# Attention, experts and channel mix on one core: row sums from a column of ones, float32 probabilities for the whole first token tile, overlapping query columns, and new order tables

## The chip, the cores and the metric

The kernel runs on one core of a Trainium2 chip. It is one program that works on five engines: PE (TensorE, the matrix multiplier; its weight loads, which overlap its multiplies, are listed as PEld), DVE (VectorE), ACT (ScalarE), POOL (GpSimd) and SP (SyncE, which here only starts DMA transfers). Each engine runs its own queue of instructions in order and waits at semaphores for the others. The metric is the device time of one execution in microseconds (us).

## The reference, cut to what matters

Three layers follow each other on 2 batches of 768 tokens. The first is attention with 8 heads of 64 columns, in which a token sees only the keys that fall in its own hash bucket; the second a mixture of 4 experts, each a causal attention of its own; the third a channel mix with a shift by one token.

```python
# 1. bucketed attention: q, k, v are (2, 8, 768, 64), proj is (64, 6)
mask = q_bucket[:, :, :, None] == k_bucket[:, :, None, :]   # bucket: signs of q @ proj, k @ proj
scores = where(mask, 0.125 * q @ k.T, -1e9)
attn = exp(scores - max(scores)); attn = attn / (sum(attn) + 1e-09)
x = attn @ v                                                # heads side by side: (2, 768, 512)
# 2. four experts, each token takes two of them with weights w
a = exp(causal scores of x @ wq[e], x @ wk[e] - max); a /= sum(a) + 1e-09
out += w * (a @ (x @ wv[e]) @ wo[e])
# 3. channel mix, xk and xr mix a token with the one before it by mu_k, mu_r
k = maximum(xk @ w_k, 0); v = k * k @ w_v                   # w_k 512x1024, w_v 1024x512
return sigmoid(xr @ w_r) * v                                # w_r 512x512
```

## The kernel before

**Tiles.** The 1536 tokens are 12 tiles of 128 (i = 0 to 11, six to a batch). Each tile goes through the three layers in turn: for each of the 8 heads a score matrix of 128 tokens by 768 keys (`s`), its exponentials (`P`), and the product with the values (`x`); then the expert projections (`qk`, `vg`), the expert scores (`se`), their exponentials (`P_m` for one expert, `P_m_p` for two side by side) and products (`y`, `o`); then the channel mix (`h` hidden, `r` gate, `v` down), and a store to `out`.

**Numbers in two halves.** To keep float32 accuracy at 16-bit matmul speed, a float32 tile is split into a 16-bit "hi" part and the 16-bit rest "lo". Keys, queries, values and all weights are split this way when they are first used (`nak`, `nbk` for keys, `naq`, `nbq` for queries, `v` for values, and for weights `raw`, `wd`, then `WK`, `WV`, `WR`). A hi part is a copy that ACT, DVE or POOL can make; a lo part is a subtraction on DVE or POOL.

**One head of the attention.** PE multiplies `s`. DVE scales it into `P` and takes the row maximum `mx` in the same instruction (TENSOR_SCALAR_CACHE_REDUCE). ACT takes the exponential in place, and its `accum_out` gives the row sum `sm` (a second instruction, ACTIVATION_READ_ACCUMULATOR, follows each). ACT or POOL makes the hi half `PHL`, POOL the lo half, one DMA transpose on SP's queue turns both into `PT`, and PE multiplies 18 times per head with 64 columns of values. For eight pairs of tile and head (the set `F32T`) it goes another way: PE turns `P` in float32 by six transposes (`tp`), ACT copies them out of PSUM (`PF`), and PE multiplies in float32; no half, no DMA transpose. When all heads of a tile are done, DVE adds 1e-9 to the eight sums, takes reciprocals, and multiplies all 512 columns by them (`x32`, shown as `x<-x,rs`); PE then turns `x32` (`tr_x<-ident,x`) for the expert projections.

**What sets the order.** Nothing is issued where it stands in the code. A recorder (`Program`) keeps every instruction as an operation; a long table (ORDER) gives the order of issue, a second one (HOMES) the buffer of each tile, and a third (ENGINES) the engine of each hi part. All are then issued by one function, and so every row of the profile has line L225; the rows are told apart by tile names. Within an engine the order is fixed, so an instruction that waits holds up all that stand behind it.

**Start.** SP issues the loads of keys, queries and weights in the order of the table. The ACT queue issues the small ones: the projection twice (`pr32`, upper and lower 64 rows), `mur` and `muk` (512 numbers each, scattered one by one over 128 rows), the constants (identities and causal mask) and `ties`. ACT's first table load of an activation function stands behind these.

Of the kernel before, what the change touches and what calls it, by code (L numbers as in the profile page):

```python
# [25 lines left out]
SMQ = 64.0  # L26
# [20 lines left out]
F32T = {(i, h) for i in range(4) for h in (0, 1)}  # L47
# [205 lines left out]
def tile_lsh_moe_mix(  # L253
# [61 lines left out]
    consts = cp.tile([P, 3 * P], F16, name="consts")  # L315
    nc.scalar.dma_start(consts, consts_in[:, :3 * P])
    ident16 = consts[:, :P]
    ident = consts[:, P:2 * P].bitcast(BF16)
    causal = consts[:, 2 * P:3 * P].bitcast(BF16)
    ident32 = cp.tile([P, P], F32, name="ident32")  # L320
    nc.gpsimd.tensor_copy(ident32, ident16)
    pr32 = cp.tile([P, NB], F32, name="pr32")
# [5 lines left out]
    ties = cp.tile([P, E, E], F32, name="ties")  # L328
    muk = cp.tile([P, NC], F32, name="muk")
    mur = cp.tile([P, NC], F32, name="mur")  # L330

    def late_consts():
        nc.scalar.dma_start(ties, ties_in)
        nc.gpsimd.tensor_scalar(ties, ties, -(2.0 ** -120), 1.0, op0=OP.mult, op1=OP.mult)
        nc.scalar.dma_start(muk, mu_k.rearrange("(c p) -> p c", p=P))
        nc.scalar.dma_start(mur, mu_r.rearrange("(c p) -> p c", p=P))
# [18 lines left out]
    def turn(dst, src, nm, by_dma=False, engs="vv"):  # L355
# [4 lines left out]
        n = src.shape[1] // P  # L360
# [6 lines left out]
        for j in range(2):  # L367
            for c in range(hn):
                nc.tensor.transpose(pt[j][:, c * P:(c + 1) * P], src[:, (j * hn + c) * P:(j * hn + c + 1) * P], ident16)
# [104 lines left out]
    def key_steps(b, g):  # L474
# [4 lines left out]
        def load():  # L479
# [3 lines left out]
            st["v"] = kp.tile([P, 2, G, NT, D], F16, tag="v", name=f"v_{nm}")  # L483
# [3 lines left out]
        def half(j):  # L487
# [25 lines left out]
        def vals(j):  # L513
# [6 lines left out]
            vh, vl = st["v"][:, 0, 2 * j:2 * j + 2], st["v"][:, 1, 2 * j:2 * j + 2]  # L520
# [8 lines left out]
    NBQ = cp.tile([P, H, P], F16, name="nbq")  # L529
    nc.gpsimd.memset(NBQ[:, :, D + 2 * NB:], 0.0)  # L530

    def query_steps(i):
# [4 lines left out]
        def prep():  # L537
# [3 lines left out]
            st["na"] = na = sp.tile([P, H, P], F16, tag="b2", bufs=NB2, name=f"naq_{i}")  # L541
            nb = NBQ
            nc.scalar.activation(na[:, :, :D], q32, AF.Copy, scale=SQ)
            nc.vector.scalar_tensor_tensor(na[:, :, D:], q32, SQ, na[:, :, :D], op0=OP.mult, op1=OP.subtract)
# [502 lines left out]
```

## Time and profile before

| | before |
|---|---|
| median of 3 runs | 453.11 us (453.09 to 453.51) |
| the profiled execution, device time | 451.91 us |
| its span in the profile | 450.1 us (1.8 us lie around it) |
| busy PE / PEld | 419.1 us (93%) / 323.0 us (72%) |
| busy DVE / ACT / POOL | 350.3 (78%) / 317.9 (71%) / 349.7 us (78%) |
| TensorE clock granted | 1.00 of full speed in every stretch, which is 2.4 GHz |
| read / written in device memory | 22.14 MB / 3.15 MB |

Busy time is the time in which an engine has at least one instruction in work. On PE, where one multiply begins before the last has ended, the time from start to start tells more than the length of one. The sums further on are made against the profiled execution; the median of the runs lies 1.20 us above it.

### The profile page before, as it was taken

The page shows a single profiled execution, that of the slowest core. Times are in us where ns is not written, and L with a number is a line of the kernel's source. Part 1 is how long each engine was busy: PE and PEld are TensorE (multiplying, and loading weights), DVE is VectorE, ACT ScalarE, POOL GpSimd, SP SyncE. Part 2 cuts the span into 40 slices and gives each one's busy share as a digit, 9 for nine tenths or more (in the row PEclk, how much of TensorE's full clock was granted, in tenths as well). Part 3 has the DMA queues.
Part 4 walks back from the last instruction along what each step waited for, and adds up shares of the span by engine and source line. Part 5 has one row for each costly group of instructions (what it writes and reads, how often), then busy time and mean ns, then how long its engine had stood idle before and what let it go on. Part 6 is the DMA issues. An engine that isn't in the chain of part 4 may idle for free.

```text
span 450.1 us, 14852 instructions
## 1 busy us (share of the span) xinstructions
PE 419.1 (93%) x5984; PEld 323.0 (72%) x5984; DVE 350.3 (78%) x900; ACT 317.9 (71%) x617; POOL 349.7 (78%) x364
## 2 busy tenths in 40 slices
PE   0776798999999999999999999999999999999996
PEld 0655686888787677885778778777678868577672
DVE  1999999999999888998878878768758765655522
ACT  2898999998988795877786666668667636662220
POOL 4898998998999786899988899978987953844020
PEclk9999999999999999999999999999999999999999
DMA  8989999999999999498899999997998885328201
GB/s 247 233 234 221 251 207 243 196 194 257 199 161 212 192 220 229 107 169 145 144 158 199 184 155 198 179 161 114 188 158 161 125 146 83 83 58 169 60 1 70
DMA packets 227157, 75.54 MB, mean 168 GB/s; under 512 B 218512, under 2 KB 222736, under 8 KB 227088
## 3 DMA queue, kind: packets, MB, share of 16 engines
q1 hardware_dynamic: 225584, 74.48, 87.9%
q8 instruction: 47, 0.77, 0.7%
q10 hardware_dynamic: 1504, 0.11, 0.2%
q14 instruction: 22, 0.18, 0.1%
HBM read 22.14 MB, written 3.15 MB: 56 GB/s over the span
## 4 chain that ended last, share of the span: by engine, by line
PE 69%; DVE 11%; POOL 3%; issue 3%; ACT 2%; DMA 1%; DVEq 0%; POOLq 0%; ACTq 0%
PE v L225 13%; PE h L225 11%; PE x L225 9%; PE s L225 9%; PE r L225 6%; PE qk L225 6%; PE o L225 4%; DVE P L225 3%; PE se L225 3%; PE vg L225 3%; PE y L225 3%; DVE v L225 2%; POOL PHL L225 1%; PE tr_y L225 1%; DMA PT<-PHL 1%
## 5 line engine op out<-in xcount | busy, mean ns | idle before, releaser
L225 POOL TENSOR_TENSOR PHL<-P,PHL 128x768 f16<-128x768 f32 x88 | 146.7, 1674 | 9.5 <-ACT PHL L225 3.6
L225 ACT ACTIVATE P<-P,mx 128x768 f32<-128x768 f32 x96 | 89.2, 931 | 20.4 <-DVE P L225 16.9
L225 DVE TENSOR_SCALAR_CACHE_REDUCE P<-s 128x768 f32<-128x768 f32 x96 | 90.7, 950 | 8.3 <-PE s L225 6.0
L225 PE MATMUL s<-y,x 128*128 128x384 f16 x384 | 76.3, 326 | 7.4 <-DVE P L225 3.7
L225 PE MATMUL h<-mk,WK 128*128 128x128 f16 x1152 | 75.0, 219 | 0.0
L225 PEld LDWEIGHTS <-WK 128*128 128x128 f16 x1152 | 67.9, 98 | 6.2 <-DVE lg L225 0.4
L225 PEld LDWEIGHTS <-PT 128*128 128x128 f16 x1584 | 54.5, 98 | 8.9 <-DMA PT<-PHL 2.2
L225 PE MATMUL x<-v,PT 128*128 128x64 f16 x1584 | 58.0, 193 | 1.9 <-DMA PT<-PHL 1.9
L225 PEld LDWEIGHTS <-x 128*128 128x128 f16 x480 | 38.0, 98 | 27.4 <-issue 7.3
L225 PE MATMUL v<-WV,k2h 128*128 128x512 f16 x192 | 57.1, 379 | 0.0
L225 POOL TENSOR_SCALAR PHL<-P 128x768 f16<-128x768 f32 x50 | 42.8, 858 | 7.3 <-ACT P L225 4.1
L225 POOL TENSOR_TENSOR PHL_m<-P_m,PHL_m 128x512 f16<-128x512 f32 (+2 forms) x24 | 33.5, 1405 | 8.9 <-ACT PHL_m L225 8.4
L225 PE MATMUL r<-WR,mr 128*128 128x512 f16 x144 | 36.0, 379 | 0.8 <-DVE k2l L225 0.8
L225 PE MATMUL qk<-xT,WQK 128*128 128x128 f16 x576 | 36.6, 219 | 0.1
L225 PE MATMUL v<-WV,k2l 128*128 128x512 f16 x96 | 36.4, 379 | 0.0
L225 ACT ACTIVATE t<-h 128x512 f32<-128x512 f32 x24 | 14.2, 594 | 28.0 <-PE h L225 27.9
L225 PEld LDWEIGHTS <-WQK 128*128 128x128 f16 x576 | 33.3, 98 | 1.0 <-DVE xT L225 0.4
L225 ACT ACTIVATE PHL<-P 128x768 f16<-128x768 f32 x38 | 31.6, 838 | 2.2 <-ACT P L225 0.9
L225 DVE SCALAR_TENSOR_TENSOR h<-h,t 128x512 f32<-128x512 f32 x24 | 16.7, 694 | 18.8 <-ACT t L225 18.7
L225 PEld LDWEIGHTS <-k2h 128*128 128x128 f16 x192 | 16.8, 98 | 13.8 <-issue 0.7
L225 ACT ACTIVATE P_m<-P_m,bias_m 128x512 f32<-128x512 f32 (+2 forms) x24 | 19.7, 821 | 8.7 <-DVE P_m L225 8.7
L225 ACT ACT_TABLE_LOAD x16 | 20.5, 1283 | 6.5 <-DMA pr<-in_proj_dram 5.0
(172 smaller groups left out, 882.9 us busy)
## 6 DMA issues: line engine op xcount, KB each, us to landing
raw_k<-in_moe_w_k_dram SPq DMA_DIRECT2D x8, 512.0 KB, 4.8
raw_v<-in_moe_w_v_dram SPq DMA_DIRECT2D x8, 512.0 KB, 4.4
k<-in_k_dram SPq DMA_DIRECT2D x8, 384.0 KB, 5.1
q<-in_q_dram SPq DMA_DIRECT2D x12, 256.0 KB, 4.7
v<-in_v_dram SPq DMA_DIRECT2D x8, 384.0 KB, 4.3
out_dram<-e SPq DMA_DIRECT2D x12, 256.0 KB, 2.6
raw_r<-in_moe_w_r_dram SPq DMA_DIRECT2D x4, 512.0 KB, 4.9
PT<-PHL SPq DMA_TRANSPOSE x88, 4.6
```

The source lines that it names most:

```text
L225: getattr(getattr(self.nc, engine), method)(*[real(a) for a in args], **{k: real(a) for k, a in kw.items()})
```

## The change

Six things change together.

- **Row sums.** The hi half of the values gets a column of ones beside each 64 columns of values (`vh`, and `vnh` for the experts), so that the matmuls with it have 65 columns and the row sum of the probabilities appears in PSUM beside the product. The exponentials lose `accum_out` (88 of 96 in the attention, all 48 of the experts). The normalisation reads the sums from PSUM, and is done in two halves of four heads (`fin_half`), each with a PSUM tile of its own.
- **Float32 heads.** `F32T` has heads 0 and 1 of tiles 0 to 3 before, and all 8 heads of tile 0 now.
- **Queries.** For tiles 0 to 7 one tile `NQ` holds lo, hi and hash marks side by side, and the two turned operands are overlapping columns of it. The hi half is copied once, not twice.
- **Constants.** Identities, mask and `ties` are built on POOL (memset and AFFINE_SELECT). `mu_k` and `mu_r` are loaded as rows of 128 numbers and turned by PE (`tr_mu`). The two loads of `pr32` stand together at the head of the ACT queue.
- **Last tile.** The down projection of tile 11 is done in two halves of 256 columns, each with its own product and store.
- **Tables.** ORDER, HOMES and ENGINES are new. ENGINES gives 52 of the attention's hi halves to ACT and 36 to POOL, where 38 and 50 stood.

```diff
-F32T = {(i, h) for i in range(4) for h in (0, 1)}
+F32T = {(0, h) for h in range(8)}
...
-    consts = cp.tile([P, 3 * P], F16, name="consts")
-    nc.scalar.dma_start(consts, consts_in[:, :3 * P])
...
+    def pattern(name, shape, dt, steps, rows, op, fill):
+        t = cp.tile(shape, dt, name=name)
+        nc.gpsimd.memset(t, 0.0)
+        nc.gpsimd.affine_select(t, t, pattern=steps, compare_op=op, fill=fill, base=0, channel_multiplier=rows)
+        return t
...
     def late_consts():
-        nc.scalar.dma_start(ties, ties_in)
...
-        nc.scalar.dma_start(muk, mu_k.rearrange("(c p) -> p c", p=P))
-        nc.scalar.dma_start(mur, mu_r.rearrange("(c p) -> p c", p=P))
+        rows = sp.tile([P, P], F32, tag="b2", bufs=NB2, name="mu_rows")
+        nc.scalar.dma_start(rows[0:NC, :], mu_k.rearrange("(c p) -> c p", p=P))
+        nc.scalar.dma_start(rows[NC:2 * NC, :], mu_r.rearrange("(c p) -> c p", p=P))
+        pt = dps("tr_mu")[:, :2 * NC]
+        nc.tensor.transpose(pt, rows[0:2 * NC, :], ident32[0:2 * NC, 0:2 * NC])
+        hi_part("a", mu, pt)
...
+            st["vh"] = kp.tile([P, G, NT, D + 2], F16, tag="vh", name=f"vh_{nm}")
+            nc.gpsimd.memset(st["vh"][:, :, :, D:], 1.0)
...
-            nc.scalar.activation(na[:, :, :D], q32, AF.Copy, scale=SQ)
-            nc.vector.scalar_tensor_tensor(na[:, :, D:], q32, SQ, na[:, :, :D], op0=OP.mult, op1=OP.subtract)
-            nc.gpsimd.tensor_scalar(nb[:, :, :D], q32, SQ, 1.0, op0=OP.mult, op1=OP.mult)
+            if i in QD:
...
+            else:
+                lo, hi = NQ[:, :, :D], NQ[:, :, D:2 * D]
+            hi_part("a", hi, q32, SQ)
+            lo_part("v", lo, q32, hi, SQ)
...
-            nc.scalar.activation(d, d, AF.Exp, bias=biases[r], scale=-1.0, accum_out=sms[r])
+            nc.scalar.activation(d, d, AF.Exp, bias=biases[r], scale=-1.0)
...
+            o1 = st["x"][:, hh, :]
             for t in range(NT):
-                nc.tensor.matmul(o, PT[:, t, :], kg["v"][:, 0, hh, t, :], start=(t == 0), stop=False)
+                nc.tensor.matmul(o1, PT[:, t, :], kg["vh"][:, hh, t, :D + 1], start=(t == 0), stop=False)
...
+        def fin_half(g):
...
+            nc.vector.tensor_scalar(rs, st["sm"][:, hs] if own[0] else x[:, :, D], 1e-9, 1.0, op0=OP.add, op1=OP.mult)
+            nc.vector.reciprocal(rs, rs)
+            nc.vector.tensor_tensor(st["x32"].rearrange("p (h d) -> p h d", d=D)[:, hs], x[:, :, :D],
+                                    rs.unsqueeze(2).to_broadcast([P, G, D]), op=OP.mult)
...
+        def down_half(j, f):
...
+            nc.vector.scalar_tensor_tensor(o, pv_, 1.0 / (ST * ST * SWV2), o, op0=OP.mult, op1=OP.mult)
+            LOADS.dma_start(out[b, s0:s0 + P, js], o)
...
 ORDER = """
-c-jrsg8~@F5&*!x-CJC2+qP}nwr$(CZ5wS+#6}z2DPlX#d-D^6&>jHVfC7OBg8)$=3sizwP!zI4IcNvjAR-7jXbTabB+P?oFaU}{RLB7gIiWa|hg?trazhE|4-23S{OY
```

What stands on the queues, read from the order of instructions. Names carry buffer numbers behind them, and a "32" in a name is left out (`x_3` below is `x32_3`).

The head of the ACT queue, before:

```order
L225 DMA pr_72<-in_proj_dram 64x6
L225 DMA mur<-in_moe_mu_r_dram 128x4x1
L225 DMA consts<-in_consts_dram 128x384
L225 DMA ties<-in_ties_dram 128x16
L225 DMA pr_72<-in_proj_dram 64x6
L225 ACT_TABLE_LOAD
L225 ACTIVATE nak_0_0_85<-k_0_0_0_80 128x12x64
```

and now:

```order
L225 DMA pr_77<-in_proj_dram 64x6 x2
L225 DMA mu_rows<-in_moe_mu_r_dram 4x128
L225 DMA mu_rows<-in_moe_mu_k_dram 4x128
L225 ACT_TABLE_LOAD
L225 ACTIVATE nbq<-q_0_100 128x8x64
L225 ACTIVATE wd_k_0_119<-raw_k_0_113 128x512
L225 ACTIVATE mu<-tr_mu 128x8
```

The second projection load moved from fifth place to second, three loads went, and the first copy is one of queries where it was one of keys.

The head of DVE's queue, before:

```order
L225 CAST prhl<-pr_72 128x6
L225 SCALAR_TENSOR_TENSOR nak_0_0_85<-k_0_0_0_80,nak_0_0_85 128x12x64
L225 SCALAR_TENSOR_TENSOR naq_103<-q_0_95,naq_103 128x8x64
L225 TENSOR_TENSOR prhl<-pr_72,prhl 128x6
L225 COPY x_0_136<-tr_x_0_130 128x512
```

and now:

```order
L225 CAST prhl<-pr_77 128x6
L225 TENSOR_TENSOR prhl<-pr_77,prhl 128x6
L225 SCALAR_TENSOR_TENSOR nbq<-q_0_100,nbq 128x8x64
L225 SCALAR_TENSOR_TENSOR wd_k_0_119<-raw_k_0_113,wd_k_0_119 128x512
L225 COPY x_0_129<-tr_x_0_106 128x512
L225 SCALAR_TENSOR_TENSOR wd_k_0_119<-raw_k_0_113,wd_k_0_119 128x512
L225 SCALAR_TENSOR_TENSOR nak_0_0_136<-k_0_0_0_132,nak_0_0_136 128x12x64
```

The cast of the projection still stands first; behind it queries and a weight now come ahead of the first keys.

DVE's queue from the end of tile 3's normalisation on, before (204 instructions stand ahead of the first row, from the top of the queue):

```order
L225 TENSOR_TENSOR x_3_2330<-x_2046,rs_2077 128x512
L225 TENSOR_SCALAR P_6_2337,mx_2126<-s_6_2316 128x768
L225 SCALAR_TENSOR_TENSOR WV_3_2340<-wd_v_0_2231,WV_3_2340 128x512
L225 TENSOR_TENSOR xT_2343<-tr_x_2332,xT_2343 128x512
L225 TENSOR_SCALAR P_m_p_2365,bias_m_2_2366<-se_1_2353 128x384
```

and now (200 stand ahead):

```order
L225 TENSOR_TENSOR x_3_2043<-x_0_2056,rs_2034 128x256
L225 TENSOR_SCALAR P_7_2239,mx_1962<-s_7_2182 128x768
L225 TENSOR_SCALAR lg_2253,gm_2254<-vg_2216 128x4
L225 SCALAR_TENSOR_TENSOR WV_1_2191<-wd_v_0_2041,WV_1_2191 128x512
L225 TENSOR_TENSOR xT_2276<-tr_x_2232,xT_2276 128x512
L225 SCALAR_TENSOR_TENSOR wd_r_0_2331<-raw_r_0_2107,wd_r_0_2331 128x512
```

The one multiply of 512 columns is now the second of two with 256, with four instructions fewer ahead of it; among these, the ones that split `w_v` and `w_r` (`wd_v`, `wd_r`, `WV`, `WR`) fell from 24 to 14.

## Rows read from the trace of the kernel before

**Rows 1.** Windows: stretch, length, busy of PE, PEld, DVE, ACT, POOL, clock, DMA.

```profile
10.00:40.00 30.00, 21.34 (x246) 16.48 (x247) 29.40 (x61) 26.82 (x48) 26.96 (x28) 1.00 0.99 225
40.00:80.00 40.00, 33.79 (x500) 27.91 (x500) 39.09 (x95) 36.93 (x82) 37.66 (x40) 1.00 1.13 231
80.00:120.00 40.00, 39.44 (x591) 33.98 (x589) 39.29 (x106) 38.14 (x84) 38.05 (x41) 1.00 1.08 215
120.00:180.00 60.00, 59.93 (x895) 45.96 (x893) 54.55 (x146) 48.77 (x93) 51.35 (x55) 1.00 1.08 204
```

**Rows 2.** Timeline 0 to 13 us: start us, us, engine, instruction.

```profile
0.72 0.55 ACTq L225 DMA_DIRECT2D pr<-in_proj_dram  x1
4.50 0.49 ACTq L225 DMA_DIRECT2D pr<-in_proj_dram  x1
10.04 0.37 DVE L225 CAST prhl<-pr 128x6 f16<-128x6 f32 x1 [10.04 <-DMA pr<-in_proj_dram]
10.14 0.96 DVE L225 SCALAR_TENSOR_TENSOR nak<-k,nak 128x768 f16<-128x768 f32 x1
11.16 0.82 PE L225 MATMUL tr_y<-consts,nak 128*128 128x128 f16 x6 [11.16 <-DMA w_qk<-in_moe_wk_dram]
```

**Rows 3.** Timelines around 99, 119 and 150 us: normalisation of tiles 2 to 4, its transposes.

```profile
99.72 0.64 PE L225 MATMUL tr_x<-ident,x 128*128 128x128 f32 x4
118.76 0.68 DVE L225 TENSOR_TENSOR x<-x,rs 128x512 f32<-128x512 f32 x1
119.73 0.60 PE L225 MATMUL tr_x<-ident,x 128*128 128x128 f32 x4
149.45 0.68 DVE L225 TENSOR_TENSOR x<-x,rs 128x512 f32<-128x512 f32 x1
161.47 0.60 PE L225 MATMUL tr_x<-ident,x 128*128 128x128 f32 x4
```

**Rows 4.** Page, part 6: DMA issues, KB each, us to landing.

```profile
k<-in_k_dram SPq DMA_DIRECT2D x8, 384.0 KB, 5.1
q<-in_q_dram SPq DMA_DIRECT2D x12, 256.0 KB, 4.7
```

**Rows 5.** Lines by form, DVE: count, busy us, mean ns, idle before.

```profile
L225 DVE TENSOR_SCALAR_CACHE_REDUCE P<-s 128x768 f32<-128x768 f32 x96 | 90.7, 950 | 8.3 <-PE s L225 6.0 <-ACT P L225 1.5 <-DMA PT<-PHL 0.2
L225 DVE SCALAR_TENSOR_TENSOR wd_v<-raw_v,wd_v 128x512 uint32<-128x512 uint32 x16 | 11.1, 692 | 0.8 <-issue 0.6
L225 DVE TENSOR_TENSOR x<-x,rs 128x512 f32<-128x512 f32 x12 | 8.2, 686 | 3.0 <-PE x L225 3.0
L225 DVE TENSOR_TENSOR y<-y,rse 128x256 f32<-128x256 f32 x12 | 5.0, 420 | 1.4 <-PE y L225 1.2
L225 DVE RECIPROCAL rs<-rs 128x8 f32<-128x8 f32 x12 | 2.4, 196 | 0.1
```

**Rows 6.** Timeline 108 to 113 us, DVE: how far one instruction overlaps the next.

```profile
109.05 0.41 DVE L225 TENSOR_SCALAR_CACHE_REDUCE P_m_p<-se 128x256 f32<-128x256 f32 x1
109.39 0.41 DVE L225 TENSOR_SCALAR_CACHE_REDUCE P_m_p<-se 128x256 f32<-128x256 f32 x1
```

**Rows 7.** Timeline 144 to 147.2 us, PE: runs of matmuls at full rate.

```profile
144.25 1.50 PE L225 MATMUL h<-mk,WK 128*128 128x128 f16 x24
146.24 1.16 PE L225 MATMUL x<-v,PT 128*128 128x64 f16 x34
```

**Rows 8.** Timeline 59.5 to 63 us, ACT: an exponential and two copies.

```profile
59.97 0.95 ACT L225 ACTIVATE P<-P,mx 128x768 f32<-128x768 f32 x1
60.88 1.58 ACT L225 ACTIVATE PHL<-P 128x768 f16<-128x768 f32 x2
```

**Rows 9.** Lines by form, ACT: the copies of turned float32 probabilities.

```profile
L225 ACT ACTIVATE PF<-tp 128x384 f32<-128x384 f32 x15 | 7.1, 485 | 0.1
```

**Rows 10.** Timeline 441 to 450.1 us: the end.

```profile
446.33 0.69 DVE L225 SCALAR_TENSOR_TENSOR e<-v,e 128x512 f32<-128x512 f32 x1 [1.96 <-PE v L225]
```

**Rows 11.** Tile nak: duration ns min/median/max of the DVE instruction.

```profile
L225 DVE SCALAR_TENSOR_TENSOR nak<-k,nak x8: 947/958/1571, 10.1 to 178.4; 128x768 f16<-128x768 f32 x8
```

More of the change, by code (lines that the diff above doesn't have):

```diff
@@ L359, in turn @@
             return
-        n = src.shape[1] // P
+        n = dst.shape[1]
         hn = n // 2
@@ L368, in turn @@
             for c in range(hn):
-                nc.tensor.transpose(pt[j][:, c * P:(c + 1) * P], src[:, (j * hn + c) * P:(j * hn + c + 1) * P], ident16)
+                t = j * hn + c
+                nc.tensor.transpose(pt[j][:, c * P:(c + 1) * P],
+                                    src[:, t, :] if len(src.shape) == 3 else src[:, t * P:(t + 1) * P], ident16)
             o, pj = dst[:, j * hn:(j + 1) * hn, :], pt[j].rearrange("p (n s) -> p n s", s=P)
@@ L528, in tile_lsh_moe_mix @@
     QX, QS_ = {}, {}
-    NBQ = cp.tile([P, H, P], F16, name="nbq")
-    nc.gpsimd.memset(NBQ[:, :, D + 2 * NB:], 0.0)
+    NQ = cp.tile([P, H, 3 * D], F16, name="nbq")
+    nc.gpsimd.memset(NQ[:, :, 2 * D + 2 * NB:], 0.0)
     def query_steps(i):
@@ L616, in score @@
             if h == 0:
-                st["sm"] = sp.tile([P, H], F32, tag="sm", name=f"sm_{i}")
+                if any((i, hh) in F32T for hh in range(H)):
+                    st["sm"] = sp.tile([P, H], F32, tag="sm", name=f"sm_{i}")
                 st["mx"] = sp.tile([P, H], F32, tag="mx", name=f"mx_{i}")
@@ L664, in lsh_steps @@
                 steps.append(lambda h=h: pv(h - LAG))
+            if h >= LAG and (h - LAG) % G == G - 1:
+                steps.append(lambda h=h: fin_half((h - LAG) // G))
         steps.append(lambda: fin())
@@ L684, in proj_qk @@
                 KV[b] = (kp.tile([P, 2, EP, S], F16, tag="kT", bufs=1, name=f"kT_{b}"),
-                         kp.tile([P, NT, 2, E * D], F16, tag="vn", bufs=1, name=f"vn_{b}"))
+                         kp.tile([P, NT, E, D + 2], F16, tag="vnh", bufs=1, name=f"vnh_{b}"),
+                         kp.tile([P, NT, E, D], F16, tag="vnl", bufs=1, name=f"vnl_{b}"))
+                nc.gpsimd.memset(KV[b][1][:, :, :, D:], 1.0)
             kT = KV[b][0]
@@ L739, in proj_v @@
             nc.gpsimd.tensor_scalar(gs, gs, 1e-9, 1.0, op0=OP.add, op1=OP.mult)
-            st["sm"] = sp.tile([P, E], F32, tag="sme", name=f"sme_{i}")
         def score(c):
@@ L775, in score @@
                 es = (2 * c, 2 * c + 1)
-                PT = softmax_pair(Sv, n, 0.125 / (SMQ * SMQ), [st["sm"][:, e:e + 1] for e in es],
+                PT = softmax_pair(Sv, n, 0.125 / (SMQ * SMQ),
                                   [sp.tile([P, 1], F32, tag="bias", bufs=4, name=f"bias_m{i}_{e}") for e in es],
@@ L904, in gate @@
                 nc.scalar.activation(e, pr, AF.Sigmoid, scale=1.0 / (SX2 * SWR))
+        def down_half(j, f):
+            need(W)
+            js = slice(j * DM // 2, (j + 1) * DM // 2)
+            if f == 0:
+                st["pv"] = dps(f"v_{i}_{j}", [P, DM // 2])
+            pv_, k2 = st["pv"], st["k2"]
+            nc.tensor.matmul(pv_, k2[0][:, f, :], WV2[f][:, 0, js], start=(f == 0), stop=False)
+            nc.tensor.matmul(pv_, k2[0][:, f, :], WV2[f][:, 1, js], start=False, stop=False)
+            nc.tensor.matmul(pv_, k2[1][:, f, :], WV2[f][:, 0, js], start=False, stop=(f == NF - 1))
+            if f < NF - 1:
+                return
+            o = st["e"][:, js]
+            nc.vector.scalar_tensor_tensor(o, pv_, 1.0 / (ST * ST * SWV2), o, op0=OP.mult, op1=OP.mult)
+            LOADS.dma_start(out[b, s0:s0 + P, js], o)
         def down(f):
@@ L921, in mix_steps @@
                                   + [lambda c=c: gate(c) for c in range(NC)]
-                                  + [lambda f=f: hidden(f) for f in range(4, NF)] + [lambda f=f: down(f) for f in range(NF)])]
+                                  + [lambda f=f: hidden(f) for f in range(4, NF)]
+                                  + ([lambda f=f: down(f) for f in range(NF)] if i < NU - 1 else
+                                     [lambda j=j, f=f: down_half(j, f) for j in range(2) for f in range(NF)]))]
     W = weight_steps()
```

206 lines of the change are left out of this document (107 added, 99 removed).

## The prediction

> **What bounds the kernel now.** I read the windows by stage first. From 80 us on PE is busy nearly all the time, 39.44 of 40 us and then 59.93 of 60 us, while in 10 to 40 us it is busy 21.34 of 30 and in 40 to 80 us 33.79 of 40 [rows 1]. DVE is the reverse: 29.40 of 30, 39.09 of 40 and 39.29 of 40 us up to 120, then 54.55 of 60. So there are two regimes. Until about 120 us DVE never rests and sets the pace; after that PE never rests, and an instruction saved elsewhere buys nothing. The clock granted to PE is 1.00 in every stretch, so no clock enters the sum.
>
> Next the timeline, for where each regime begins. DVE's first instruction is the cast of the projection, at 10.04 us, and it waits for the second projection load, which the ACT queue issues only at 4.50 us; DVE's next, the lo part of the first keys, follows at 10.14, and PE's first transpose at 11.16 [rows 2]. The wait table puts PE's 11.16 us down to a weight load, but the transposes read `nak`, whose lo part ends at 11.10; it is DVE that released it.
>
> Then the seam. Normalisation of tile 3 on DVE runs from 118.76 for 0.68 us, and PE starts the transposes that need it at 119.73, 0.29 us after its end. Tile 2's transposes start at 99.72. Tile 4's normalisation ends at 150.13, but PE only comes to it at 161.47, so 11.3 us of slack lie there [rows 3]. Tile 3 is thus the last delivery of DVE for which PE waits long. The end moves by what PE's waiting up to tile 3's transposes loses, which is how much earlier DVE delivers, less how much less work PE has ahead of it, unless tile 4 then comes late.
>
> **The start.** The ACT queue now issues four loads of a few rows, the two projections first, at 0.72 and, by the 0.55 us of the first issue, about 1.3 us, in place of 4.50 [rows 2]. DVE can cast at some 6 us. What it does next hangs on loads: the first queries are now first on SP's queue (5.4 us by the 0.72 of an issue and the 4.7 to landing, then a hi copy on ACT, under the 0.73 of a wider one [rows 8]), then a weight, then keys, which land some 5.1 us after an issue [rows 4]. The first keys are now third on SP's queue, at about 1.7 us, so land at about 7 and are ready in both halves near 9, by which time DVE has some 3 us of work behind it. Before, the first useful work began at 10.14 with 0.1 us of work behind it. I bound the gain between 3 us (the third and fourth pair of keys land one after the other, and DVE waits once more) and 5.5 us (it never waits), and take 4.0. PE's first instruction is now a transpose of the `mu` rows, which waits for the fourth load of the ACT queue, issued by about 2.9 us and landing by 8.0 if a few rows take as long as keys do; then the query transposes start there and the gain is at its low end. Building constants on POOL costs two AFFINE_SELECTs that the trace does not show, between nothing and the 0.95 us of the longest instruction in [rows 8] each; POOL had nothing to do then but memsets, and PE needs the identity only near 6 us, so I take nothing.
>
> **DVE's work up to tile 3.** By the order, 204 instructions stand ahead of the last multiply of tile 3's normalisation before, 200 now. I price each by its mean less 0.07 us, since one of 0.41 us starts 0.34 us after the last [rows 6].
> - The splits of `w_v` and `w_r` fall from 24 to 14: 10 x 0.62 = -6.2 us (0.692 less 0.07) [rows 5]. They are not gone, but done later.
> - One block of the channel mix (`h`, `k2l`) and one cast of `xT`, 512 wide, move behind: 3 x 0.62 = -1.9. Two reductions `P_m_p` of 384 columns move behind: between the 0.42 of 256 and the 0.69 of 512 columns, 2 x 0.48 = -1.0.
> - Three reductions of `P` come ahead: 3 x 0.88 = +2.6 [rows 5].
> - Normalisation in halves: 8 multiplies of 256 columns (0.420 less 0.07) for 4 of 512 (0.686 less 0.07), +0.3; 8 sums and 8 reciprocals for 4 and 4, at 0.1 to 0.2 us each [rows 5], +1.2.
> - Four more copies of transposes (+1.5) and some ten fewer small instructions (-1.5) cancel.
>
> The sum is -5.0 us; with the start, tile 3 is delivered 9.0 us earlier. The same list for tile 2 gives +0.4, so 3.6 earlier.
>
> **PE's work up to there.** Ahead of tile 3's transposes PE has 48 hidden matmuls fewer. 24 take 1.50 us, of which the last hangs over by some 0.2, so one costs about 0.056: -2.7. Eight score matmuls of 384 columns come ahead, eight expert scores and 16 small transposes and hash products go: +1.3 - 1.1 - 0.6. A matmul of 64 columns costs (1.16 - 0.19) / 33 = 0.0294, one of 128 0.0557, so 0.41 ns for a column [rows 7]. In all -2.9 us. PE's waiting up to tile 3 falls by 9.0 - 2.9 = 6.1 us. At tile 2 it falls by 3.6 + 1.6 = 5.2, since PE has 1.6 us more to do there. Between those two transposes PE spent 20.0 us [rows 3] on 18.4 us of work, so tile 2 was 1.6 us less tight, and tile 3 still decides.
>
> **What stands next to be late.** By the order PE has 18.9 us less work ahead of tile 4's transposes (96 hidden, 20 score, 24 output matmuls and others moved behind them) and DVE 10.8 us less. PE gets there at 161.47 - 18.9 - 6.1 = 136.5, DVE delivers at 150.13 - 10.8 - 4.0 = 135.3. The 11.3 us of slack shrink to 1.2, enough if each step holds.
>
> **What PE does more.** 1392 matmuls get a 65th column (1056 of 1584 in the attention, 336 of 504 in the experts). The trace has none of 65; one costs between a 64 column matmul and a 128 column one, 0 to 26 ns more, so 0 to 36 us in all. Being one column from the near end, I take 0.41 ns, 0.6 us. The Trainium skill, "TensorE: Matmul & The Clock Gate", section "Back-to-back issue gap", lists a floor of about 25 ns for all widths up to 64 and N/2.4 + 2.5 ns above; by that step the column would cost 4.6 ns and 6.4 us in all. The trace's 29.4 ns at 64 columns is already on the sloped line and not on that floor. The float32 path has the same 48 transposes and 48 matmuls as before, only elsewhere. The last tile's halves add 24 matmuls, about 0.1 us, and at the end a multiply of 256 columns (0.42) stands where one of 512 (0.69) did [rows 10], with half the bytes to store: -0.4.
>
> **What costs or gains nothing.** An exponential with its accumulator read holds ACT 0.91 us, a copy of the same shape 0.73 [rows 8]: 136 of them give back 25 us of ACT, and POOL loses some 16 us by the moved hi halves. Both lie under DVE until 120 us (ACT is busy 38.14 and POOL 38.05 of 40 there, DVE 39.29) and under PE after. The cover is that DVE never rests; DVE's own total stays within 1.1 us.
>
> **Sum.** -6.1 + 0.6 + 0.1 - 0.4 = -5.8 against the profiled 451.9: 446.1. The median stood 1.2 above the profiled execution, so 447.3.
>
> **The rivals.**
> 1. Less than the forecast: DVE gains its start, but loses what came off its work to waits for loads or PE (the 1.2 us at tile 4 are used up; in 10 to 120 us it now rests only 2.2 us [rows 1], and denser is hardly possible). The gain is then 3 us, 450.1 by the median. For it: the gain of 5 us in work rests on a reshuffle. Against: nothing that moved behind is needed by tile 4.
> 2. More: the relief of ACT and POOL speeds DVE. Its subtractions of keys take 0.947 to 1.571 us [rows 11], the long ones while POOL works. If values and queries run short too, and DVE's 2.2 us of rest go, another 3 to 4 us come off: 443.5. Against: POOL is still full up to 120 us.
> 3. Slower: the float32 heads of tile 0. All eight now go through 16 copies `PF` on ACT within about 25 us, each 0.485 us [rows 9] and each standing in ACT's queue behind exponentials of 0.93; DVE, PE and the turned tiles' four PSUM buffers hang on them, where DMA transposes carried six of eight heads. If each copy makes PE or DVE wait w, the cost is 16 w; it overturns the gain of 5.8 from w = 0.36 us on, and at w = 0.7 (most of one exponential each) the time is 453.1 - 5.8 + 11 = 458. Against: before, the two copies for one head waited little, only 0.1 us in 15 [rows 9], and PE has other heads' scores to do meanwhile.
> 4. The change doesn't gain: the 65th column is dear. If each costs a sixth of the 26 ns between the two widths measured, 4.4 ns, 6.1 us take the place of 0.6: 452.8. Against: the two rows lie on one line that needs no step. The Trainium skill's table, named above, has that step at 64 columns, and by its 6.4 us the time would be 453.1.
>
> **Chances.** Forecast 0.42 (its own range 445.5 to 449); rival 1, 0.22; rival 2, 0.19; rival 3, 0.11; rival 4, 0.06. 0.2%, 0.9 us, is about what a measurement of this kernel can tell from no change. Rivals 1 and 2 with the forecast are faster, 0.83; rival 4 is about the same, 0.06; rival 3 slower, 0.11. The range takes in rivals 1 and 2 with their bounds and leaves out 3 and the outer part of 4: 441.5 to 452.
>
> **What would show it.** DVE's first instruction at about 6 us and PE's near 6 to 8, not 10.04 and 11.16. PE's transposes of tile 3 some 9 us earlier (near 111), tile 4's near 136, waiting under 1 us. No accumulator reads but eight behind the attention's exponentials and none in the experts. A run of 65 and 64 column matmuls at 29.4 to 30 ns. The last multiply 0.42 us long. I am wrong if PE's busy share in 10 to 80 us doesn't rise, if the waits for `PF` or `tp` in 25 to 60 us add up to more than 5 us, or if PE after 120 us has rests that it had not.

## The result and the profile after

The changed kernel takes 456.03 us (median of ten runs, 454.68 to 458.54), the one before 453.35 (ten runs beside them): ratio 1.0068, 95% interval 1.0045 to 1.009. It is slower by 0.7% where a gain of 5.8 us was forecast. The profiled execution of the changed kernel is its longest, 458.54 us with a span of 456.8, so its losses stand 2.5 us above the median's.

The windows by stage of the changed kernel (columns as in [rows 1]):

```profile
0.00:10.00 10.00, 0.60 (x5) 0.61 (x6) 1.65 (x4) 2.87 (x5) 5.92 (x20) 1.00 0.82 249
10.00:40.00 30.00, 26.58 (x298) 21.86 (x296) 29.07 (x64) 28.60 (x56) 23.47 (x30) 1.00 0.94 229
40.00:80.00 40.00, 35.99 (x499) 29.81 (x498) 39.15 (x90) 36.31 (x64) 37.37 (x36) 1.00 1.04 224
80.00:120.00 40.00, 34.34 (x550) 27.05 (x547) 36.09 (x107) 37.28 (x62) 33.31 (x34) 1.00 1.12 197
120.00:180.00 60.00, 56.75 (x813) 42.29 (x811) 52.49 (x134) 49.11 (x76) 49.66 (x52) 1.00 1.07 212
180.00:280.00 100.00, 97.56 (x1537) 78.48 (x1536) 82.36 (x223) 77.23 (x116) 87.73 (x86) 1.00 0.95 159
280.00:380.00 100.00, 98.63 (x1416) 73.58 (x1414) 72.30 (x207) 64.77 (x97) 75.78 (x76) 1.00 0.90 152
```

and the last two of the kernel before:

```profile
180.00:280.00 100.00, 98.56 (x1551) 78.18 (x1549) 85.44 (x222) 74.87 (x144) 89.15 (x86) 1.00 0.96 161
280.00:380.00 100.00, 99.78 (x1481) 76.06 (x1478) 69.16 (x194) 65.12 (x127) 79.96 (x81) 1.00 0.91 149
```

Read PE's column against [rows 1]. Up to 80 us PE is busy 63.17 us where it was 55.13 (nothing before 10 us): 8.0 us gained, more than the forecast asked for. From 80 to 180 us it is busy 91.09 of 100 where it was 99.37: 8.3 us given back. Another 2.2 go by 380. The clock is 1.00 in all these windows, so no clock moved the end. DVE lost its density as well, 36.09 of 40 us where it had 39.29: from 80 to 120 us neither engine is full, so something else may be late. The tile view of the turned probabilities `PT` from 80 to 160 us names one such thing. Before:

```profile
L225 SPq DMA_TRANSPOSE PT<-PHL x22: 1302/1857/2750, 79.7 to 159.4; - x22
```

and after, with the idle time of PE and of its weight loads before they read `PT`, added up (us, times):

```profile
L225 SPq DMA_TRANSPOSE PT<-PHL x23: 1303/1487/4942, 79.6 to 159.5; - x23
  DMA PT<-PHL: 5.8, 9
```

Before, that list of idle times is empty: no product in this stretch waited for its transpose. The 5.8 us now count a weight load and the product behind it one by one; PE's own wait table for 80 to 160 us (us, times, longest) tells what PE lost. Before:

```profile
PE s L225 <- DVE P L225: 0.3, 1, 0.3
PE tp L225 <- DVE WR L225: 0.3, 1, 0.3
```

and after, but for two rows of 0.6 and 0.2 us on DVE:

```profile
PE x L225 <- DMA PT<-PHL: 2.2, 4, 1.1
PE s L225 <- DVE P L225: 1.8, 2, 1.2
PE y L225 <- DMA PT_m<-PHL_m: 1.3, 1, 1.3
PE x L225 <- DVE WV L225: 1.3, 1, 1.3
PE y L225 <- DMA PT_m_p<-PHL_m_p: 1.1, 2, 0.6
```

So PE waits 8.5 us where it waited 0.6: 4.6 us for turned probabilities (four products of the attention, three of the experts) and 3.9 for DVE. SP's timeline shows the queue behind the transposes, before:

```profile
108.70 0.91 SPq L225 DMA_DIRECT2D q<-in_q_dram  x1
110.65 1.47 SPq L225 DMA_TRANSPOSE PT<-PHL  x1
113.11 2.09 SPq L225 DMA_TRANSPOSE PT_m_p<-PHL_m_p  x1
```

and after:

```profile
101.44 8.10 SPq L225 DMA_TRANSPOSE PT<-PHL  x4
109.59 1.01 SPq L225 DMA_DIRECT2D raw_r<-in_moe_w_r_dram  x1
110.70 4.04 SPq L225 DMA_TRANSPOSE PT_m_p<-PHL_m_p  x2
114.83 4.80 SPq L225 DMA_TRANSPOSE PT<-PHL  x2
```

Before, SP rests about 1 us between these issues (109.61 to 110.65, 112.12 to 113.11). After, each issue begins 0.05 to 0.1 us behind the last. Added up over the issues from 80 to 160 us, SP is held for some 62 of 80 us before and 75 after. On PE products of tile 3 start as their transposes land, two of them here:

```profile
99.63 0.20 PE L225 MATMUL x<-vh,PT 128*128 128x65 f16 x1 [0.30 <-DMA PT<-PHL]
107.24 0.20 PE L225 MATMUL x<-vh,PT 128*128 128x65 f16 x1 [1.14 <-DMA PT<-PHL]
```

Tile 2's, 3's and 4's transposes of normalised rows, the marks of [rows 3], now start here:

```profile
98.06 0.63 PE L225 MATMUL tr_x<-ident,x 128*128 128x128 f32 x4
114.52 0.60 PE L225 MATMUL tr_x<-ident,x 128*128 128x128 f32 x4
141.98 0.60 PE L225 MATMUL tr_x<-ident,x 128*128 128x128 f32 x4
```

They are 1.7, 5.2 and 19.5 us earlier; 3.6, 9.0 (DVE's delivery) and 25 were forecast. And the prediction's own sign "PE after 120 us has rests that it had not" came true: PE is busy 56.75 of 60 us from 120 to 180 where it was 59.93.

### The profile page after: what moved, and what is told of

The parts are those of the page before. It is cut to its first block, busy times and chain, and to the rows that moved or that the text cites. A ratio compares the mean times of both kernels' runs of the same rounds, so it can differ in the third digit from the quotient of the medians.

```text
span 456.8 us, 14817 instructions
## 1 busy us (share of the span) xinstructions
PE 423.8 (93%) x6009; PEld 327.7 (72%) x6009; DVE 350.6 (77%) x916; ACT 322.4 (71%) x511; POOL 336.5 (74%) x354
## 4 chain that ended last, share of the span: by engine, by line
PE 49%; DVE 6%; DMA 3%; issue 2%; ACT 2%; POOL 1%; DVEq 0%; POOLq 0%; ACTq 0%
PE v L225 11%; PE h L225 10%; PE s L225 5%; PE r L225 5%; PE x L225 4%; PE qk L225 4%; DMA PT<-PHL 3%; PE y L225 2%; PE vg L225 2%; PE se L225 2%; PE o L225 2%; DVE P L225 1%; POOL PHL L225 1%; DVE vl L225 1%; PE tr_y L225 1%
## 5 line engine op out<-in xcount | busy, mean ns | idle before, releaser
L225 ACT ACTIVATE P<-P,mx 128x768 f32<-128x768 f32 x96 | 88.6, 935 | 19.5 <-DVE P L225 11.7
L225 PE MATMUL h<-mk,WK 128*128 128x128 f16 x1152 | 73.5, 219 | 0.1
L225 PE MATMUL x<-vh,PT 128*128 128x65 f16 x1056 | 58.7, 194 | 5.6 <-DMA PT<-PHL 3.5
L225 PE MATMUL v<-WV,k2h 128*128 128x512 f16 (+1 forms) x208 | 57.6, 363 | 0.0
L225 ACT ACTIVATE PHL<-P 128x768 f16<-128x768 f32 x52 | 43.5, 840 | 3.7 <-POOL gt L225 1.2
L225 PE MATMUL x<-vl,PT 128*128 128x64 f16 x528 | 43.4, 193 | 0.0
L225 POOL TENSOR_SCALAR PHL<-P 128x768 f16<-128x768 f32 x36 | 31.2, 867 | 11.7 <-ACT P L225 9.4
L225 PE MATMUL qk<-xT,WQK 128*128 128x128 f16 x576 | 38.2, 219 | 0.9 <-DVE x L225 0.6
L225 PE MATMUL v<-WV,k2l 128*128 128x512 f16 (+1 forms) x104 | 37.7, 363 | 0.0
L225 PEld LDWEIGHTS <-k2h 128*128 128x128 f16 x208 | 18.6, 98 | 13.6 <-issue 0.4
```

Of the source, the lines that this page charges most:

```text
L225: getattr(getattr(self.nc, engine), method)(*[real(a) for a in args], **{k: real(a) for k, a in kw.items()})
```

## The experiments

Ratios are to the kernel before, run beside it on the same chip, with 95% intervals; the changed kernel stands at 1.0068.

**The start alone.** The kernel before, with the second projection load moved to second place on the ACT queue.

```diff
+        self.order.remove(second)
+        self.order.insert(self.order.index(first) + 1, second)
```

> The kernel before with the second load of the projection moved to second place on the ACT queue, nothing else. If the start is worth in the end what it is worth there, DVE starts near 7 us and the time falls by about 3 us, to 450 us. If DVE's early work is given back at a later wait, 453 us as before.

453.32 us, 0.9995 [0.9973, 1.0017]. DVE's first rows:

```profile
5.54 0.17 DVE L229 CAST prhl<-pr 128x6 f16<-128x6 f32 x1 [5.54 <-DMA pr<-in_proj_dram]
7.00 0.96 DVE L229 SCALAR_TENSOR_TENSOR nak<-k,nak 128x768 f16<-128x768 f32 x1 [1.29 <-ACT nak L229]
10.63 0.42 DVE L229 COPY x<-tr_x 128x512 f16<-128x512 f16 x1 [2.00 <-PE tr_x L229]
```

The cast comes 4.5 us earlier, but DVE then waits for ACT's copy of the keys and for PE, and PE's first scores come at 23.29 us where they came at 23.34. By itself the earlier projection load gains PE nothing.

**The engines of the hi halves.** The changed kernel, with the hi halves of tiles 2 to 4 on the engines that they had before.

```diff
+        hi = {2: "AAGGGGAA", 3: "AGGGAAGA", 4: "AGGGAGGG"}
...
+                o.move(hi[int(part[1])][int(part[2])])
```

> The changed kernel with the hi halves of tiles 2 to 4 made by the engines that made them before (17 of 24 heads change hands at most, most of them from ACT back to POOL), order untouched. Theory 'SP queue' (from 84 to 126 us SP issues one DMA transpose after another with gaps of 0.1 us, and PE waits for what lands): a half that is ready earlier or later by a microsecond changes nothing, 455 to 457 us. Theory 'halves on ACT' (POOL now waits 19.8 us for ACT's halves, 3.6 before, and so the lo halves and the transposes are late): 3 us or more come back, 453 us or less.

457.64 us, 1.0094 [1.0066, 1.0123]. PE is busy 34.43 of 40 us in 80 to 120, as in the changed kernel. The halves of these tiles on ACT are not the cause.

**Half the transposes, heads 2 to 7 of tiles 1 to 3,** in the changed kernel and, as a control, in the one before. Only the lo half is turned, and it is multiplied in the hi half's place too; in the changed kernel 1.0 stands for 1e-9 in these row sums.

```diff
-        nc.sync.dma_start_transpose(PT, PHL)
+        if nm in HALF:
+            nc.sync.dma_start_transpose(PT[:, :NT], PHL[:, n:])
+        else:
+            nc.sync.dma_start_transpose(PT, PHL)
```

> The changed kernel; for heads 2 to 7 of tiles 1 to 3 only the lo half is turned by the DMA (half the bytes of 18 transposes), and PE multiplies that half twice, so that PE, ACT, POOL and DVE have the same instructions and the transpose still waits for the lo half; the row sums of these tiles get 1.0 added in place of 1e-9. Theory 'SP queue': SP gets room, PE's waits between 80 and 130 us (some 6 us) shrink by half or more, 450 to 453 us. Theory 'halves on ACT': the transposes are not what is late, 455 to 457 us.

> The kernel before with the same edit to the same 18 heads. PE waits under 1 us for turned probabilities after 80 us there and SP's queue has gaps, so theory 'SP queue' expects less than in the changed kernel: 451.5 to 453.5 us, by up to 1.5 us through earlier landings before 80 us. If it gains as much as the changed kernel does (3 us or more), the saturation is not particular to the change.

454.68 us, 1.0029 [1.0006, 1.0052]; the control 452.45, 0.9976 [0.9957, 0.9995]. Both gain some 0.3%, so by the time this pair does not tell the theories apart. The trace of the changed kernel so halved says why. No product waits for `PT` any more from 80 to 160 us, and the transposes of tiles 3 and 4 start at 111.81 and 138.75. But PE now waits 3.0 us for the experts' `PT_m` and `PT_m_p`, which this run leaves whole (2.4 in the changed kernel), and tile 5's transposes start at 185.99, 47.2 us behind tile 4's; in the changed kernel 47.0 us lie between them (188.98).

**Half the transposes, wider.** As above, and also all heads of tiles 4 and 5 and the experts of tiles 0 to 3, which takes in the experts' transposes that PE waited for.

> The changed kernel with the lo half alone turned by DMA for heads 2 to 7 of tiles 1 to 3, all heads of tiles 4 and 5, and all experts of tiles 0 to 3 (the turned half is multiplied twice, 1.0 in place of 1e-9 is added to the sums concerned; every engine keeps its instructions). In the changed kernel PE waits 7.6 us for turned probabilities after 60 us, 2.1 in the kernel before. Theory 'transposes': all of that goes, and half_turn_after's 454.7 falls on to 450 to 452.5. Theory 'DVE and PSUM' (PE waits for buffers that DVE has yet to read, 7.8 us between 60 and 160 us, 1.1 before): one wait takes the other's place, 454 to 455.5.

> The same edit in the kernel before, as the yardstick. By the 2.1 us of such waits there at most 2 us, 451 to 453; if it gains as much as the changed kernel, transposes cost both alike.

450.79 us (450.47 to 451.07), 0.9934 [0.9912, 0.9955]; the control 452.12, 0.997 [0.9954, 0.9987]. The changed kernel gains 1.34%, some 6 us, the one before 0.3%, 1.4 us. Of the changed kernel so halved, the tile view of `PT` (80 to 160 us) and two windows:

```profile
L225 SPq DMA_TRANSPOSE PT<-PHL x26: 1209/1212/2097, 79.5 to 159.6; - x26
```

```profile
80.00:120.00 40.00, 37.09 (x603) 30.37 (x603) 38.85 (x120) 39.65 (x67) 36.19 (x37) 1.00 0.87 155
120.00:180.00 60.00, 59.59 (x927) 45.78 (x924) 55.63 (x142) 51.08 (x78) 53.25 (x56) 1.00 0.79 146
```

The 7.6 us that the expectation names are 5.9 in PE's own wait table from 60 us on, 4.6 of them from 80 to 160. With the halving no wait for turned probabilities is left there; 3.6 us of waits for DVE are. SP is held for some 54 of these 80 us. PE is busy 96.68 us of the 100 from 80 to 180 where it was 91.09, and the transposes of tiles 3, 4 and 5 start here:

```profile
111.93 0.60 PE L225 MATMUL tr_x<-ident,x 128*128 128x128 f32 x4
137.47 0.60 PE L225 MATMUL tr_x<-ident,x 128*128 128x128 f32 x4
181.05 0.61 PE L225 MATMUL tr_x<-ident,x 128*128 128x128 f32 x4
```

The forecast had "near 111" and "near 136". What kept tiles 3 and 4 from coming nearly when they were forecast was the turning of the probabilities by DMA. That alone was not the loss, as the run before shows; with the experts' transposes halved as well, only 43.6 us lie between tiles 4 and 5, and the order is faster than the old one.

**Six transposes cut to a twelfth:** heads 0 and 1 of tiles 1 to 3, those that the move of the float32 heads added; the control cuts heads 2 and 3 of the same tiles in the kernel before. One block of 128 columns is turned and used for all products.

```diff
+        if nm in LITTLE:
+            nc.sync.dma_start_transpose(PT[:, :1], PHL[:, 2 * n - P:])
+        else:
+            nc.sync.dma_start_transpose(PT, PHL)
```

> The changed kernel, where heads 0 and 1 of tiles 1 to 3 (the six whose probabilities PE turned in float32 before and a DMA transpose turns now) transpose only one block of 128 columns of twelve, used for every product, and 1.0 stands for 1e-9 in their row sums; everything else, the number of transposes too, is as in the changed kernel. Theory A, these six transposes on SP's queue are what makes the turned probabilities late: most of what halving all of them gave back comes back, ratio 0.996 to 1.000, and PE waits for DMA data under 2 us in 60 to 160. Rival B, they are late because PE and DVE now arrive earlier at all tiles and the queue has no slack anywhere: the gain is in proportion to the queue time taken off (5.5 transposes' worth; nine transposes' worth gave 0.4%), so 0.2%, ratio 1.004 to 1.006.

> Control: the kernel before with the same cut for six of its transposes, heads 2 and 3 of tiles 1 to 3. In it turned probabilities made PE wait only 2 us in 60 to 160. Theory A and rival B both: 0.997 to 1.000. A gain as large as that of the changed kernel's six would say that shorter transposes speed this kernel in any order, and that neither theory is needed.

457.22 us, 1.0085 [1.006, 1.0111]; the control 452.09, 0.9985 [0.9969, 1.0001]. Nothing comes back in time, so theory A is not borne out: PE still waits 3.1 us for turned probabilities from 80 to 160 us (4.6 in the changed kernel). But the test takes bytes off the queue and not time. The shortest of these issues still holds SP for 1.12 us, and SP is held for some 77 of the 80 us. What the six places in the queue cost stays untested.

**Nine weight loads issued by ACT** instead of SP, in the changed kernel.

```diff
+        for o in late[:9]:
+            o.eng, o.calls = "ACT", [("scalar",) + o.calls[0][1:]]
```

> The changed kernel, with the first nine weight loads from the first of w_v on (raw_v and one raw_r, issued by SP between 83 and 160 us, between transposes) issued by the ACT queue instead, at the same places of the order. Theory C, the turned probabilities are late because SP issues one thing after another: SP gets back some 0.9 us per load, 5 us by 136 us, and the time falls to 1.001 to 1.004. Theory D, the transfers themselves are the limit (the DMA engines), or ACT pays for the issues what SP saves: 1.006 or more, and SP's transposes grow longer by what the loads freed.

460.41 us, 1.0158 [1.0124, 1.0192]; the profiled execution, 457.27 us, is the shortest. Theory D's number, not C's. PE still waits for `PT`, 3.0 us in 3 times from 80 to 160 us. There a transpose's issue takes 2.376 us in the median where it took 1.487, and it lands 5.8 us after its issue where it took 4.9; SP is held for some 73 of the 80 us. What the loads freed on SP the transposes took up, and the last product of tile 4 starts at 138.2 us where it started at 138.6. ACT's own price for the loads is in the time too, and the two are not told apart.

**Row sums from the exponentials again** in the changed kernel (accumulator reads on ACT, 64 columns in every product), with the order, buffers and engines of the changed kernel.

```diff
-            nc.scalar.activation(d, d, AF.Exp, bias=biases[r], scale=-1.0)
+            nc.scalar.activation(d, d, AF.Exp, bias=biases[r], scale=-1.0, accum_out=sums[r])
...
-            nc.vector.tensor_scalar(rs, st["sm"][:, hs] if own[0] else x[:, :, D], 1e-9, 1.0, op0=OP.add, op1=OP.mult)
+            nc.vector.tensor_scalar(rs, st["sm"][:, hs] if own[0] else SUMS[:, i, hs], 1e-9, 1.0, op0=OP.add, op1=OP.mult)
```

> The changed kernel with the row sums taken from the exponentials again (accumulator reads behind each on ACT) and 64 columns in every product with values; the order, buffers and engines are the changed kernel's. If ACT's relief was worth nothing and the 65th column costs what the trace says (0.6 us): 1.005 to 1.008, the changed kernel's own. If ACT's 25 us of relief had a worth of its own in the new order: slower, 1.010 or more. If the 65th column is dear (rival 4 of the prediction, 6 us): faster, 0.993 to 0.996.

463.88 us, 1.0248 [1.022, 1.0277]: 1.8% slower than the changed kernel. But a small row had grown. DVE's addition of 1e-9 in this kernel, with one of its instances and POOL's work beside it:

```profile
L225 DVE TENSOR_SCALAR rs<-sums x22: 154/548/1449, 65.1 to 384.6; 128x4 f32<-128x4 f32 x22
98.12 1.45 DVE L225 TENSOR_SCALAR rs<-sums 128x4 f32<-128x4 f32 x1
94.49 5.05 POOL L225 TENSOR_TENSOR PHL<-P,PHL 128x768 f16<-128x768 f32 x3 [0.55 <-ACT PHL L225]
```

Four columns take up to 1.45 us, and that one ends at 99.57, when POOL's subtractions end (99.54). So the run was made again with the addition in the form of the kernel before, which reduces into a ninth column:

```diff
+                nc.vector.tensor_scalar(rs, SUMS[:, i, hs], 1e-9, None, op0=OP.add, op1=OP.min, accum_out=st["rs"][:, H:])
```

> The changed kernel with its row sums from the exponentials again, as in sums_from_exp, but the normalisation adds 1e-9 in the form that the kernel before had (with a reduction into a ninth column, 155 ns there), not in the plain form, which took 626 ns on average from SBUF in sums_from_exp and ended with a POOL instruction (98.12 to 99.57 beside POOL's to 99.54). If the loss of that run was this plain form: the 22 instructions fall back to 155 ns and the time to 1.004 to 1.010, so that the row sums neither gain nor lose much by themselves. If ACT's relief has a worth of its own in the new order: still 1.015 or more with the instructions at 155 ns. If reading the sums from PSUM behind the product costs (DVE waits 5.8 us for it in the changed kernel): under 1.004.

461.0 us, 1.0141 [1.0101, 1.0182], and the addition takes 148 ns:

```profile
L225 DVE TENSOR_SCALAR_CACHE_REDUCE rs<-sums x22: 139/148/154, 64.3 to 384.0; 128x4 f32<-128x4 f32 x22
```

So 1.1% of the 1.8% were the form of 22 small instructions. The other 0.7%, some 3 us, is what the row sums beside the values gain in this order; the two intervals, 1.0045 to 1.009 and 1.0101 to 1.0182, do not meet. Not all of it need be ACT: the granted clock of this run is 0.96 in 40 to 80 us, where the changed kernel had 1.00.

**No accumulator reads in the old order.** The kernel before, without accumulator reads behind 136 exponentials, its divisors taken from the product's PSUM tile.

> The kernel before (its float32 heads, buffers, engines and 64-column products) with the row sums' part alone on the engines ACT and DVE: no accumulator read behind 136 exponentials, and the normalisation takes its divisor from the PSUM tile of the product (its first column, at least 768) after the last product, as the changed kernel does, so the two or three small DVE instructions of each normalisation stand behind the last product where the old order had them earlier. It leaves out the row sums. If ACT's relief is worth nothing in the old order, as the prediction had it (ACT hidden under DVE and PE): 0.997 to 1.003. If it is worth there what the run with sums from the exponentials showed in the new order (1.8%): 0.980 to 0.985, and the loss lies wholly in the other parts (float32 heads and tables). If DVE's small instructions on the path from product to transposes cost (12 times 0.4 us): up to 1.010.

466.19 us, 1.0267 [1.0242, 1.0292]: above all three expectations. DVE now waits 9.5 us (10 times) for PE before `rs`, where it waited 3.0 before the multiply [rows 5]. Its queue runs in order, and I had put the small instructions directly behind the last product and not directly ahead of the multiply, so these waits hold up all that stands behind them. How much of the 12 us they make was not separated, and the worth of ACT's relief in the old order stays open.

**Buffers.** Five runs were to put single parts of the change into the other kernel's order, with a sixth as their control. Each needed new buffers for some tiles.

> The kernel before with its own order and engines, and only the buffers of the tiles (the HOMES table) given out anew by the rule that the next three kernels need: the oldest free buffer of the smallest size that fits. A control: if buffers don't matter it stays within 0.3% of the kernel before, 452 to 454.5 us; if they do, the next three are to be read against this one.

> Row sums by the column of ones, normalisation in halves, constants built on POOL, rows of mu turned by PE, both projection loads first and the last tile in halves, all in the ORDER and on the ENGINES of the kernel before (new operations stand beside those they belong to); float32 heads and queries as before. Theory 'table' (the parts are worth little, the new order with its float32 heads loses): 451.5 to 454 us. Theory 'row sums' (DVE now waits for PE before each normalisation, 5.8 us in the changed kernel, and that is the loss): 455 us or more.

> The reverse: row sums from the exponentials, whole normalisation, loaded constants, two query copies and the whole last tile as before, but in the ORDER and on the ENGINES of the changed kernel and with its float32 heads (all eight of tile 0). Theory 'table': the loss is still there, 455 to 458 us. Theory 'row sums': the loss is gone, 451 to 454 us.

> The kernel before with one part: the float32 heads are all eight of tile 0 in place of heads 0 and 1 of tiles 0 to 3, in the order before (turned heads beside their exponentials; the product of a head that is now turned by DMA comes up to 50 operations later, one split of values earlier). Theory 'float32 heads' (six transposes fewer while DMA has room, six more for tiles 1 to 3, where SP's queue is full): 455 us or more. Theory 'table' in the narrow sense (the order alone): 452 to 454.5 us.

The control, the kernel before with nothing but its buffers reassigned, took 562.14 us, 1.2399 [1.2364, 1.2434]; DVE alone waits 34.0 us there to write `P` until a transpose has read the buffer. The three beside it took 581.98, 571.86 and 562.88, so they say nothing of the parts. Two were made again with only 46 and 103 of 1279 tiles moved:

> f32_old_order again, now with every tile in its old buffer but 46 of 1279 (new tiles and those in their way). Theory 'float32 heads': with the order before, tiles 1 to 3 have eight transposes each in place of six, and the time rises to 455 or more. Theory 'order': 452 to 454.5.

> old_parts_new_order again, with the changed kernel's buffers kept for all but 103 of 1279 tiles. Theory 'order and float32 heads': the loss stays without any of the other parts, 455 to 459. Theory 'row sums' (DVE waits for PE, two PSUM tiles for one): 451 to 454.

493.58 us (1.0875 [1.0846, 1.0905]) and 489.0 (1.0775 [1.0742, 1.0807]): still too far off to tell the parts apart.

## Why the prediction was wrong, step by step

**The start** was right in direction and too large: the first casts stand at 7.15 us, not about 6, and PE's first instruction at 9.40, later than the 6 to 8 named.

```profile
7.15 0.17 DVE L225 CAST prhl<-pr 128x6 f16<-128x6 f32 x1 [7.15 <-DMA pr<-in_proj_dram]
9.40 0.24 PE L225 MATMUL tr_mu<-ident,mu_rows 8*128 8x8 f32 x1 [9.40 <-DMA mu_rows<-in_moe_mu_k_dram]
9.57 0.61 PE L225 MATMUL tr_x<-ident,nbq 128*128 128x128 f16 x4
```

The `mu` rows held PE, as the low end of that bound had it. PE's first scores come at 21.04 us, 2.3 earlier where 4.0 were taken, outside the bounds of 3 to 5.5. The forecast took the late projection load for what held the start; moved forward by itself, that load gained PE nothing (23.29).

**DVE and PE up to 80 us** went the way of the forecast: PE's busy time rose by 8.0 us, and the sign of being wrong "PE's busy share in 10 to 80 us doesn't rise" did not show. In the list of PE's work ahead of tile 3 the terms add up to -3.1 and not to -2.9 us; that is 0.2 us of the forecast.

**The step that failed** is "what stands next to be late". It set DVE's delivery of tile 4 (135.3) against PE's arrival (136.5), called the slack of 1.2 us enough, and left SP's queue out. Tile 4's transposes start at 141.98, 5.5 us behind that, and from 80 to 160 us PE waits the 8.5 us shown above. The order moved tile 4's products forward by what PE and DVE had ahead of them; the transposes that the products read did not come forward with them. Counted from the rows of SP's timelines, the 20th DMA transpose is issued at 92.1 us before and 92.4 after, the 32nd at 127.9 and 123.8, the 44th at 157.1 and 154.1. Tile 4 was to come 14.8 us earlier (150.13 to 135.3). The sum had no term for the transposes, since in the trace of before PE's whole wait table has one wait for `PT`, of 1.9 us; that slack the new order spent. The wide halving shows the larger part of the cause: with it the waits for turned probabilities, 4.6 us, are gone, tiles 3 and 4 come within 1.5 us of the forecast, and the time falls by some 6 us, where the same cut gives the old order 1.4. The forecast also let tile 4's transposes stand for the end. The first halving brought them to 138.75 and gained 0.4%: behind them the experts' products wait for their transposes in turn.

That the moved float32 heads are the reason was my next theory. Six tiny transposes in their place give nothing back, but each still holds SP for 1.12 us and more, so only their bytes are cleared.

**ACT's 25 us of relief "costs or gains nothing"** was wrong by up to some 3 us in the changed kernel's favour. With the row sums from the exponentials the new order would be 1.4% slower than the old.

**The small DVE instructions** of the normalisation I priced at 0.1 to 0.2 us. From PSUM they cost that (156 ns in the median); the two of tile 0, which read SBUF in plain form, do not (0.59 and 1.12 us):

```profile
53.63 1.12 DVE L225 TENSOR_SCALAR rs<-sm 128x4 f32<-128x4 f32 x1
53.12 1.61 POOL L225 TENSOR_TENSOR WQK<-w_qk,WQK 128x512 f16<-128x512 f32 x1
```

This one ends at 54.75, POOL's subtraction at 54.73.

**The 65th column** was nearly right, and rival 4 falls: without the column the new order is not faster. A run of 65 and 64 columns goes on at 0.03 us each, and six products of 65 columns that follow each other take 0.35 us, 0.032 each:

```profile
89.44 0.19 PE L225 MATMUL x<-vh,PT 128*128 128x65 f16 x1
89.47 0.20 PE L225 MATMUL x<-vl,PT 128*128 128x64 f16 x1
89.80 0.35 PE L225 MATMUL x<-vh,PT 128*128 128x65 f16 x6
```

There the column costs 2.6 ns more than the 29.4 of [rows 7]; for the 528 such products that is some 1.4 us, where 0.6 stood for all.

The step of 4.6 ns that the Trainium skill's "TensorE: Matmul & The Clock Gate", section "Back-to-back issue gap", would give is not there; 2.6 ns is the most that shows.

**Rival 3**, slower through the float32 heads of tile 0, had the sign and not the mechanism. Waits before `PF` and `tp` are small:

```profile
L225 PE MATMUL tp<-ident,P 128*128 128x128 f32 x48 | 7.6, 277 | 1.6 <-DVE WK L225 1.0 <-DVE x L225 0.5
L225 ACT ACTIVATE PF<-tp 128x384 f32<-128x384 f32 x15 | 7.1, 535 | 0.7 <-PE tp L225 0.7
```

**Constants and tail** were right. The AFFINE_SELECTs of mask and identity cost 0.29 to 0.30 us each, the identity's on a POOL that had nothing else to do, and the last multiply is 0.42 us long:

```profile
0.99 0.29 POOL L225 TENSOR_SCALAR_AFFINE_SELECT ident<-ident 128x128 f16<-128x128 f16 x1
453.34 0.42 DVE L225 SCALAR_TENSOR_TENSOR e<-v,e 128x256 f32<-128x256 f32 x1 [1.93 <-PE v L225]
```

**What stays open.** With the transposes halved the time is 450.8, still 3.5 us above the forecast. The start fell 1.7 us short, and PE's 3.6 us of waits for DVE from 80 to 160 us (0.6 before) outlast the halving; how these add up, and why DVE is late there, was not tested. Nor is it settled what the limit of the transposes is, the DMA engines or the queue's own pace. The share of the DMA engines from 80 to 120 us was 1.08 before, 1.12 after and 0.87 with the wide halving, which cuts the bytes and the time on SP alike.

## What to carry to other kernels

When an order is made denser, list every queue that feeds the tile that moves forward, the DMA queue too, and ask of each whether its n-th transfer comes forward by as much; slack that the old trace shows there is spent, not given. A forecast that sets two engines against each other and finds 1.2 us of slack has to ask whether a third decides, as SP's queue did here. And a table of buffers is part of the speed of such a kernel: here no single part of the change could be put back by moving instructions alone.

## What the runs showed of the hardware

- A plain DVE TENSOR_SCALAR of 128x4 float32 from SBUF took 154 to 1449 ns in one kernel, and the long ones (363 ns and more) ended within 0.03 us of the end of a POOL instruction. From PSUM, or in the form with a reduction, it took 139 to 164 ns. The Trainium skill, "GPSIMD Engine Reference", section "8. Key points", says that POOL shares its SBUF interfaces with VectorE and contends with DVE instructions in a 2-port performance mode or with two SBUF inputs. These traces agree in that the long ones stood beside POOL's work (1.45 us for four columns); which mode they ran in no run here shows. In the kernel that had 22 of them the plain form cost 1.1%.
- The issue of a DMA transpose of 128x1536 fp16 held SP for 1.27 us at least and up to 4.94 us in the changed kernel, and one of a single block of 128 columns still for 1.12 us. The median of 80 to 160 us grew from 1.487 to 2.376 when nine loads went to another queue.
- The buffer table alone was worth over 100 us: 453 to 562 with the same instructions. There the granted clock fell too:

```profile
40.00:80.00 40.00, 27.61 (x274) 20.75 (x273) 27.74 (x60) 25.51 (x52) 26.17 (x24) 0.84 0.75 162
```

PE is busy 27.61 of 40 us, and the clock is 0.84 of full speed on average.
